# Chunked attention and two MLPs on one core: B and C loaded without their zeros, and the early work in a new order

## The chip, the core and the metric

The kernel runs on one core of one Trainium2 chip. Its time is the device time of one execution in microseconds (us). The core has TensorE (PE, and PEld for its weight loads), VectorE (DVE), ScalarE (ACT), GpSimd (POOL) and SyncE (SP). Most transfers between memory and the core are issued by SP, two early ones by ACT; each engine works through its own list in order.

## What is computed

Four sequences of 768 positions with 8 heads go through a decaying attention in chunks (reference, with chunks of 32), and its output through two MLPs.

```python
cum = np.cumsum(log_a_chunk, axis=-1)
L = np.exp(cum[:, :, :, None] - cum[:, :, None, :]) * causal
M = np.einsum('bhin,bhjn->bhij', Cc, Bc) * L
y[:, :, sl] = einsum(M, xc) + einsum(Cc, state) * exp(cum)[..., None]
state = exp(sum(la)) * state + sum over j of (Bc xc exp(cum_last - cum_j))
# x: (3072, 256) from y
h = x @ moe_w_in;  g = max(h, 0) + log1p(exp(-|h|));  x = g @ moe_w_out      # softplus
h = x @ moe2_w_in; g = where(h >= 1, h, where(h <= -1, 0, (h + 1)**2 / 4));  out = g @ moe2_w_out
```

## The kernel before

**Attention.** A unit u is one chunk of 128 positions of one sequence, all heads; chunk c holds the four units 4c to 4c + 3, and there are 6 chunks. For a pair of units `load_bc` brings one tile `bc` [128, 768]: 256 columns of B, then 512 columns in which C stands beside zeros. A row is one (head, n) of the 16 state entries, even rows belong to one of two heads that share a row group (e = 0), odd rows to the other (e = 1). The zeros make one matrix product in `scores_of` (L1155) give the products of both heads apart: a row adds to its own head's half and nothing to the other's. There are three buffers `bc`, taken in turn, and twelve loads of 384 KB, each by one DMA of 128 rows.

In chunk 0 the decay L of a unit is made by two matmuls (`spread`, L1115, L1116) and an exponential on ACT (`decay`, L1125); DVE multiplies it into the scores (`weigh`, L1179); POOL makes the inputs of the state (`sources`, L1131); PE then forms the unit's output and state (`out`, L1236, L1257); ACT and DVE split the output into a high and a low part (`evac`, L1289, and `ready`, L1297). In the later chunks the decay comes from a scan on DVE (L1123) over rows that were stored and loaded back (`rows`, L1093: 64 partitions per DMA, 256 KB), four units go together, and the running state is scaled by `dec`, a small table that ACT stores to memory (`store_runs`, L1072) and loads back spread over partitions (`dec`, L1100) for the second chunk.

**Weights.** They come as raw 64-bit numbers in pieces of 512 KB (`load_w`, L780), named (m, kind, j): MLP m, kind i or o (`w_in`, `w_out`), j from 0 to 7. Below i0 is (0, i, 0), o1 is (0, o, 1). The pieces are turned into float32 by `w0` (scale of the upper word, L792 to L796), `w1` (the three low bits and more, L804 on ACT), `w2` (L816 joins them on DVE), `w3` (sign, L828; not for i0, i1, o0, o1, whose `w0` is a Prelu on ACT that keeps the sign), then split into a high part (`w_hi`, L733 on ACT or L735 on DVE) and a low part (`split_w`, L966). If `w1` is on DVE, it is a shift of w0's result (L810), and `w2` is another form (L821).

**MLP.** Step s of MLP 0 takes 128 columns of the hidden layer for a whole chunk, or 256 for half a chunk in the first four steps: `up` (L1327 to L1329, three products), the gate `g` on ACT (L1422, before it once a table load, L1421), and `down` (L1451 in the first eight steps, L1463 later, where g is split too). The Prelu of i0, i1, o0, o1 must come before the table load.

**What sets the order.** `program()` lists all jobs with engine, cost in ns, due time, needs and buffers; `Jobs.order` is a list scheduler that puts them in one order, and every engine gets its part of it. Numbers steer it: costs, `RUSH` (ns by which a job is made more or less urgent), `LOW_DVE` (pieces whose `w1` is on DVE), `RUNS` (what the second half of `runs`, DVE's input to the `dec` table, waits for). Where the list leaves PE a gap in the first 26 us, filling matmuls of zeros are put in (L1494 ten at the start, L1545 later); they count as busy time.

A DMA's completion semaphore is one of eight that are used in turn, over both issuing queues: an issue waits until the transfer eight issues back has landed.

Of the kernel before, what the change touches and what calls it, by code (L numbers as in the profile page):

```python
# [14 lines left out]
NB, H, S, D, N = 4, 8, 768, 32, 16  # L15
Q = 128
HALF = 64
NC = S // Q
NU = NC * NB
# [4 lines left out]
PE, ACT, DVE, POOL, SP = "PE", "ACT", "DVE", "POOL", "SP"  # L24
# [3 lines left out]
class Jobs:  # L28
# [12 lines left out]
    def add(self, name, engine, cost=None, due=None, needs=(), takes=(), gives=(), size=0):  # L41
        assert name not in self.jobs, name
        options = engine if isinstance(engine, dict) else {engine: cost}
        takes = [t if isinstance(t, tuple) else (t,) for t in takes]
        self.jobs[name] = (options, due, [n for n in needs if n is not None], takes, list(gives), size)
# [198 lines left out]
def program():  # L244

    jobs = Jobs()
    add = jobs.add
# [36 lines left out]
    for u in range(NU):  # L284
        c, b = divmod(u, NB)
        if u % 2 == 0:
            add(("load_bc", u // 2), SP, 400, takes=["bc"], size=393e3)
        add(("load", u), SP, 400, takes=["u"], size=262e3)
        if c == 0:
            for hg in range(2):  # L290
# [252 lines left out]
}  # L543
TOGETHER = (1, 2, 3, 4, 5)
BT = 4
RUNS = [('ready', 1)]
WEIGH_POOL = []
PRELU = (2, 2)
LOW_ACT = 1
LOW_DVE = set()  # L550
PRE_FROM = 3
BIAS = {DVE: 400, POOL: 500}
PATIENCE = 0
# [21 lines left out]
N_G = 3  # L575
BEHIND = 500.0
RUSH = {
    ("cd", 7): -1000, ("decay", 5): -16000, ("load_w", 1, "i", 2): -16000, ("w1", 0, "o", 1): 16000, ("weigh", 2, 0): -16000,
}
WARM = 10  # L580
LULL = 5
# [6 lines left out]
def tile_kernel(ctx: ExitStack, tc: tile.TileContext, a0, al, bc, ub, w_in, w_out, w2_in, w2_out, out):  # L588
# [7 lines left out]
    nc = tc.nc  # L596
# [146 lines left out]
    def mine(*name):  # L743

        if name[0] in DTYPES:
            if name not in made:
                tag, i = got[name][0]
                made[name] = new(f"{tag}{i}", DTYPES[name[0]], tag)
            return [made[name]]
        return [buf(*b) for b in got[name]]  # L750
# [323 lines left out]
    @job  # L1074
    def load_bc(engine, v):

        nc.sync.dma_start(mine("load_bc", v)[0], bc[v])

    @job
    def load(engine, u):  # L1080
# [64 lines left out]
    def cb_t(u, hg):  # L1145
        bank = buf(*got["scores", last_of(u) // 2][u % 2 * 2 + hg])
        return bank[:, 256:512] if u // NB in TOGETHER and u % NB > 1 else bank
# [7 lines left out]

    def scores_of(v):

        t = mine("load_bc", v)[0]
        for p in range(2):
            for q in range(4):  # L1160
                r = slice(32 * q, 32 * q + 32)
                if 2 * v >= NB:
                    for s in range(2):
                        o = slice(HALF * s, HALF * s + HALF)
                        nc.tensor.matmul(
                            cb_t(2 * v + q // 2, q % 2)[o, p * 128:(p + 1) * 128], t[r, p * 128 + s * HALF:][:, :HALF],
                            t[r, 256 + p * 256 + s * 128:][:, :128], start=True, stop=True,
                        )
                    continue
                nc.tensor.matmul(  # L1170
                    cb_t(2 * v + q // 2, q % 2)[:, p * 256:(p + 1) * 256], t[r, p * 128:(p + 1) * 128],
                    t[r, 256 + p * 256:512 + p * 256], start=True, stop=True,
                )

    @job
# [307 lines left out]
    def finish_lo(engine, m, c, e):  # L1483
        nc.vector.tensor_tensor(
            out=xl[c][:, e], in0=mine("down", root[m, c])[e], in1=xh[c][:, e].bitcast(F32), op=ALU.subtract
        )


    with tc.manual_schedule():
        nc.scalar.preload_act_table_set("natural_log_exp_and_others")  # L1490

        nc.vector.memset(idle, 0.0)
        for i in range(WARM):
            nc.tensor.matmul(  # L1494
                buf("h", i % 2).rearrange("p (a b) -> p a b", a=4), idle, idle.unsqueeze(1).to_broadcast([128, 4, 128]),
                start=True, stop=True,
            )
# [31 lines left out]
        for r in (slice(0, HALF), slice(HALF, Q)):  # L1529
            nc.scalar.copy(eye3[r], one[r, r].unsqueeze(1).to_broadcast([HALF, H, HALF]))  # L1530
        nc.vector.tensor_reduce(
            out=of_one, in_=one.rearrange("p (k e n) -> p e k n", e=2, n=N), axis=mybir.AxisListType.XY, op=ALU.add
        )
        last = 0.0
        for name, engine, slots in order:
            got[name] = slots
# [62 lines left out]
```

## Time and profile before

| | |
|---|---|
| median of 3 runs | 555.11 us (554.71 to 556.46) |
| the profiled execution | 555.7 us, of which the span of its instructions 553.9 us |
| busy, share of the span | PE 99%, PEld 80%, DVE 79%, ACT 71%, POOL 7% |
| granted clock of TensorE | 0.999 of full speed |
| `bc` loads | 12 of 384 KB |
| DMA over the span | 116 GB/s |

Times below are us from the start of the span. An instruction's length overlaps that of the next one on its engine somewhat, so a sequence is measured from start to start. "[0.89 <-ACT gh L1422]" behind a row says that the engine stood idle for 0.89 us before it, and what released it. A busy PE may be filling matmuls.

### The profile page before, as it was taken

To read this page: it belongs to the slowest core of one execution; us is meant where nothing else is said; L and a number is where in the kernel's file an instruction comes from. 1 tells how busy PE (TensorE), PEld (TensorE's weight loads), DVE (VectorE), ACT (ScalarE), POOL (GpSimd) and SP (SyncE) were. 2 spreads that over 40 slices of the span, in tenths; PEclk is the share of its full clock that TensorE was granted. 3 is DMA by queue.
4 is the path that set the end of the run, shared out by engine and by line. 5 is a ranking of instruction groups with operands and counts; after the bars stand their busy time and mean duration, and the time that the engine had idled before them with its cause. 6 is when DMAs were issued, how large, how long until landed. Compare 5 with 4: busy or idle time off the path is not lost.

```text
span 553.9 us, 10465 instructions
## 1 busy us (share of the span) xinstructions
PE 547.3 (99%) x4001; PEld 442.8 (80%) x4001; DVE 437.5 (79%) x817; ACT 391.1 (71%) x719; POOL 38.8 (7%) x44
## 2 busy tenths in 40 slices
PE   9999999999999999999999999999999999999997
PEld 4777878888888888888888888888888888888885
DVE  7889899798856899876687898989886665876663
ACT  7969655636456667665666989786988875988783
POOL 4023110000000100001300000021310000000000
PEclk9999999999999999999999999999999999999999
DMA  7996458567232500376337324514100001100002
GB/s 271 392 238 198 130 179 235 165 213 219 90 133 76 181 1 1 113 253 227 111 116 233 108 77 145 179 38 149 44 1 0 2 0 38 39 0 1 1 1 76
DMA packets 34679, 64.73 MB, mean 117 GB/s; under 512 B 3684, under 2 KB 8164, under 8 KB 34628
## 3 DMA queue, kind: packets, MB, share of 16 engines
q1 hardware_dynamic: 34276, 63.65, 35.8%
q8 instruction: 31, 0.51, 0.4%
q10 hardware_dynamic: 352, 0.41, 0.3%
q14 instruction: 20, 0.16, 0.1%
HBM read 47.61 MB, written 16.43 MB: 116 GB/s over the span
## 4 chain that ended last, share of the span: by engine, by line
PE 93%; DMA 2%; DVE 2%; ACT 1%; SPq 1%; issue 1%; DVEq 0%; ACTq 0%
PE acc L1463 45%; PE h L1334 5%; PE h L1335 5%; PE h L1336 5%; PE z L1334 4%; PE z L1335 4%; PE z L1336 4%; PE h L1327 4%; PE h L1329 4%; PE h L1328 4%; PE acc L1451 3%; PE y L1236 1%; DMA st<-in_w_in_dram 1%; PE y L1268 1%; DMA u<-in_ub_dram 1%; PE z L1329 1%
## 5 line engine op out<-in xcount | busy, mean ns | idle before, releaser
L1437 DVE TENSOR_TENSOR gl<-g,gh 128x512 fp32r<-128x512 f32 x182 | 127.5, 705 | 55.0 <-PE acc L1463 31.1
L1463 PE MATMUL acc<-gh,woh 128*128 128x512 f32 x368 | 144.3, 392 | 0.0
L1463 PE MATMUL acc<-gh,wol 128*128 128x512 f32 x368 | 143.3, 389 | 0.0
L733 ACT CAST gh<-g 128x512 fp32r<-128x512 f32 x171 | 106.2, 621 | 26.4 <-PE acc L1463 14.2
L1463 PE MATMUL acc<-gl,woh 128*128 128x512 f32 x368 | 113.5, 389 | 0.0
L1463 PEld LDWEIGHTS acc<-gh,woh 128*128 128x128 f32 x368 | 69.1, 188 | 15.3 <-issue 0.7
L1463 PEld LDWEIGHTS acc<-gl,woh 128*128 128x128 f32 x368 | 69.1, 188 | 14.4
L1463 PEld LDWEIGHTS acc<-gh,wol 128*128 128x128 f32 x368 | 69.1, 188 | 14.1
L1422 ACT ACTIVATE g<-h 128x512 f32<-128x512 f32 x61 | 36.5, 598 | 52.5 <-PE h L1329 36.6
L1414 ACT ACTIVATE t<-t 128x512 f32<-128x512 f32 x96 | 60.9, 634 | 1.9
L1327 PE MATMUL h<-xh,wih 128*128 128x512 f32 (+1 forms) x114 | 45.8, 402 | 0.0
L1328 PE MATMUL h<-xh,wil 128*128 128x512 f32 (+1 forms) x114 | 42.8, 376 | 0.0
L1329 PE MATMUL h<-xl,wih 128*128 128x512 f32 (+1 forms) x114 | 42.8, 376 | 0.0
L1123 DVE TENSOR_TENSOR_SCAN ld<-ld,eye_t 128x512 f32<-128x512 f32 x20 | 26.5, 1364 | 2.2 <-DMA ld<-clip_z 2.2
L1407 ACT ACTIVATE t<-h 128x512 f32<-128x512 f32 x37 | 22.1, 598 | 7.5 <-PE h L1336 6.5
L1426 DVE TENSOR_TENSOR g<-h,t 128x512 f32<-128x512 f32 x37 | 25.3, 685 | 1.1 <-ACT t L1414 0.3
L1407 ACT ACTIVATE t<-z 128x512 f32<-128x512 f32 x35 | 21.0, 599 | 7.1 <-DVE g L1426 3.9
L1327 PEld LDWEIGHTS h<-xh,wih 128*128 128x128 f32 x114 | 21.5, 188 | 5.3 <-issue 1.1
L1426 DVE TENSOR_TENSOR g<-z,t 128x512 f32<-128x512 f32 x35 | 24.0, 686 | 1.5 <-ACT t L1414 0.5
L1328 PEld LDWEIGHTS h<-xh,wil 128*128 128x128 f32 x114 | 21.4, 188 | 4.6 <-issue 0.7
L1329 PEld LDWEIGHTS h<-xl,wih 128*128 128x128 f32 x114 | 21.4, 188 | 4.1
L1422 ACT ACTIVATE g<-z 128x512 f32<-128x512 f32 x19 | 11.4, 598 | 17.0 <-PE z L1336 8.5
(326 smaller groups left out, 1011.5 us busy)
## 6 DMA issues: line engine op xcount, KB each, us to landing
st<-in_w_in_dram SPq DMA_DIRECT2D x15, 512.0 KB, 5.2
st<-in_w_out_dram SPq DMA_DIRECT2D x15, 512.0 KB, 6.3
u<-in_ub_dram SPq DMA_DIRECT2D x24, 256.0 KB, 6.6
ld<-clip_z SPq DMA_DIRECT2D x20, 256.0 KB, 6.2
bc<-in_bc_dram SPq DMA_DIRECT2D x12, 384.0 KB, 5.7
pre_i<-st_plain SPq DMA_DIRECT2D x15, 256.0 KB, 2.0
pre_s<-st_plain SPq DMA_DIRECT2D x14, 192.0 KB, 5.9
pre_o<-st_plain SPq DMA_DIRECT2D x10, 256.0 KB, 2.5
```

The lines of the kernel that those rows point to most:

```text
L733: nc.scalar.copy(out, in_)
L1327: nc.tensor.matmul(o, wh, xh[c][:, k, t0:t0 + n], start=(k == 0), stop=False)
L1328: nc.tensor.matmul(o, wl, xh[c][:, k, t0:t0 + n], start=False, stop=False)
L1329: nc.tensor.matmul(o, wh, xl[c][:, k, t0:t0 + n], start=False, stop=(k == 1))
L1334: nc.tensor.matmul(bank, wh, bh, start=start, stop=False, skip_group_check=True)
L1335: nc.tensor.matmul(bank, wl, bh, start=False, stop=False, skip_group_check=True)
L1336: nc.tensor.matmul(bank, wh, bl, start=False, stop=True, skip_group_check=True)
L1414: nc.scalar.activation(out=t, in_=t, func=AF.Square, scale=0.5 / SAT, bias=0.5)
L1422: nc.scalar.activation(out=g, in_=ph, func=AF.Softplus)
L1426: nc.vector.tensor_tensor(out=g, in0=ph, in1=t, op=ALU.max)
L1437: engines[engine].tensor_tensor(out=mine("g_lo", s)[0], in0=mine("g", s)[0], in1=mine("g_hi", s)[0].bitcast(F32), op=ALU.subtract)
L1463: nc.tensor.matmul(acc_t(s, e), w, g[:, j * n:(j + 1) * n], start=(begins(e, j) and g is gh and i == 0), stop=(fc + j == NFC - 1 and g is ...
```

## The change

The array of B and C is built without zeros: for each pair of units there are two blocks of 64 rows, C then B for the rows with e = 0, B then C for those with e = 1. `load_bc` is two DMAs of 64 rows x 512 columns (128 KB each), the first into the even rows, columns 0 to 511, the second into the odd rows, columns 256 to 767. So B stands in the middle third of the tile, C of the one head in the first and of the other in the last third. `clear` zeroes the outer thirds of all rows of each of the three buffers once, ahead of its first load: buffer 0 on DVE behind the first instruction, buffer 1 on DVE behind the set-up work, buffer 2 on POOL. The moving operand of the scores takes the outer thirds (0:3:2). The scheduler's numbers are new: cost and size of `load_bc`, `RUNS`, `LOW_DVE`, `RUSH`.

```diff
-            add(("load_bc", u // 2), SP, 400, takes=["bc"], size=393e3)
+            add(("load_bc", u // 2), SP, 800, takes=["bc"], size=262e3)
...
-RUNS = [('ready', 1)]
+RUNS = [('ready', 0)]
...
-LOW_DVE = set()
+LOW_DVE = {(0, 'i', 1), (0, 'i', 5), (0, 'i', 6), (0, 'o', 1), (0, 'o', 3)}
...
-    ("cd", 7): -1000, ("decay", 5): -16000, ("load_w", 1, "i", 2): -16000, ("w1", 0, "o", 1): 16000, ("weigh", 2, 0): -16000,
+    ("decay", 5): -16000, ("load_w", 1, "i", 2): -16000, ("up", 4): 16000, ("w1", 0, "i", 7): -2000, ("w_hi", 0, "i", 2): -8000,
...
     def load_bc(engine, v):
 
-        nc.sync.dma_start(mine("load_bc", v)[0], bc[v])
+        t = mine("load_bc", v)[0].rearrange("(r e) f -> e r f", e=2)
+        for e in range(2):
+            nc.sync.dma_start(t[e][:, 256 * e:256 * e + 512], bc[v, e])
...
-        t = mine("load_bc", v)[0]
+        t = mine("load_bc", v)[0].rearrange("r (k f) -> r k f", k=3)
...
-                    cb_t(2 * v + q // 2, q % 2)[:, p * 256:(p + 1) * 256], t[r, p * 128:(p + 1) * 128],
-                    t[r, 256 + p * 256:512 + p * 256], start=True, stop=True,
+                    cb_t(2 * v + q // 2, q % 2)[:, p * 256:(p + 1) * 256], t[r, 1, p * 128:(p + 1) * 128],
+                    t[r, 0:3:2, p * 128:(p + 1) * 128], start=True, stop=True,
...
+    def clear(engine, i):
+        engine.memset(buf("bc", i).rearrange("r (k f) -> r k f", k=3)[:, 0:3:2], 0.0)
...
         nc.vector.memset(idle, 0.0)
+        clear(nc.vector, 0)
...
+        clear(nc.vector, 1)
+        clear(nc.gpsimd, 2)
         last = 0.0
```

On ACT, between the last output copy of unit 1 and the first gate, before (st1_137 holds o0, st2_138 i1, st3_139 o1; L794 is `w0`, L804 `w1`):

```order
L794 ACTIVATE w32_383<-st1_137 128x512
L804 ACTIVATE t_387<-st1_137,low_bias_73 128x512
L794 ACTIVATE w32_327<-st2_138 128x512
L804 ACTIVATE t_406<-st3_139,low_bias_73 128x512
L794 ACTIVATE w32_383<-st3_139 128x512
L804 ACTIVATE g_412<-st2_138,low_bias_73 128x512
L1421 ACT_TABLE_LOAD
L1422 ACTIVATE gh_415<-h1_210 128x512
```

and now:

```order
L794 ACTIVATE w32_390<-st1_137 128x512
L794 ACTIVATE w32_334<-st2_138 128x512
L804 ACTIVATE t_411<-st1_137,low_bias_73 128x512
L794 ACTIVATE w32_390<-st3_139 128x512
L1423 ACT_TABLE_LOAD
L1424 ACTIVATE gh_416<-h1_212 128x512
```

Two `w1`, those of i1 and o1, are no longer there; `w0` of i1 stands ahead of `w1` of o0.

On DVE, in the same stretch, before (L1179 `weigh` of units 2 and 3, L816 `w2`):

```order
L1179 TENSOR_TENSOR ld3_121<-acc1_270,ld3_121 128x512
L1179 TENSOR_TENSOR ld3_121<-h0_208,ld3_121 128x512
L816 SCALAR_TENSOR_TENSOR w32_383<-w32_383,t_387 128x512
L1179 TENSOR_TENSOR ld2_120<-acc2_285,ld2_120 128x512
L1179 TENSOR_TENSOR ld2_120<-acc0_268,ld2_120 128x512
L816 SCALAR_TENSOR_TENSOR w32_327<-w32_327,g_412 128x512
L816 SCALAR_TENSOR_TENSOR w32_383<-w32_383,t_406 128x512
L735 CAST wih1_75<-w32_327 128x512
L792 TENSOR_SCALAR w32_457<-raw_262 128x512
L966 TENSOR_TENSOR wil1_83<-w32_327,wih1_75 128x512
```

and now, one row earlier on (L1181 is `weigh`, L1299 `ready`, L810 the shift of `w1`):

```order
L1299 TENSOR_TENSOR xl0_368<-y1_269,xh0_367 128x2x128
L1181 TENSOR_TENSOR ld2_120<-acc2_291,ld2_120 128x512
L1181 TENSOR_TENSOR ld3_121<-acc1_273,ld3_121 128x512
L1181 TENSOR_TENSOR ld2_120<-acc0_271,ld2_120 128x512
L1181 TENSOR_TENSOR ld3_121<-h0_210,ld3_121 128x512
L810 TENSOR_SCALAR w32_334<-w32_334 128x512
L816 SCALAR_TENSOR_TENSOR w32_390<-w32_390,t_411 128x512
L821 SCALAR_TENSOR_TENSOR w32_334<-st2_138,w32_334 128x512
L810 TENSOR_SCALAR w32_390<-w32_390 128x512
```

The four `weigh` stand together, unit 2 and 3 in turn, and the joins and the two new shifts behind them.

On ACT, around the store and the load of the `dec` table for the second chunk, before (gh is a gate, wih and woh high parts of weights):

```order
L1072 DMA clip_p_200<-more0_148 8x8x64
L733 CAST woh0_90<-w32_383 128x512
L1422 ACTIVATE gh_551<-h0_208 128x512
L804 ACTIVATE t_561<-st1_137,low_bias_73 128x512
L804 ACTIVATE t_564<-st2_138,low_bias_73 128x512
L796 ACTIVATE w32_573<-st2_138 128x512
L1100 DMA dec0_134<-clip_p_200 128x1x512
L1422 ACTIVATE gh_580<-h1_210 128x512
L804 ACTIVATE t_583<-st3_139,low_bias_73 128x512
L796 ACTIVATE w32_586<-st3_139 128x512
```

and now:

```order
L1072 DMA clip_p_200<-more0_148 8x8x64
L796 ACTIVATE w32_492<-st1_137 128x512
L733 CAST wih3_77<-w32_472 128x512
L1424 ACTIVATE gh_567<-h1_212 128x512
L1102 DMA dec0_134<-clip_p_200 128x1x512
L804 ACTIVATE t_577<-st2_138,low_bias_73 128x512
L733 CAST woh0_90<-w32_390 128x512
L1424 ACTIVATE gh_584<-h0_210 128x512
L733 CAST woh1_91<-w32_390 128x512
L733 CAST woh2_92<-w32_492 128x512
```

The store has kept its place; the load stands two rows earlier among other work, ahead of `w1` of i4 (t_577; before t_564) and of the high parts of o0 to o3, and behind one gate more (567 is that of the fifth step, which is 580 in the list before and stands behind the load there).

On PE the fills between the first step and the outputs of units 2 and 3 go from 7 to 1, the first `down` has three steps of `up` behind it where it had two, and from then on each `up` stands one `down` earlier than before, up to the step at which the ninth and tenth `up` stood together; behind some 450 of 3,100 rows the lists agree again. On SP, the loads of rows for the second chunk (L1093) now stand ahead of the load of o4. On POOL the four low parts of o0 to o3 follow each other, and one product of MLP 0 more comes behind them.

## Rows read from the trace of the kernel before

**Rows 1.** Busy time in stretches: us from the start, length, busy time (instructions) per engine, clock, DMA share, GB/s.

```profile
5.00:10.00 5.00, 5.00 (x32) 2.41 (x30) 4.06 (x9) 3.76 (x9) 1.16 (x4) 1.00 0.88 299
...
15.00:20.00 5.00, 4.69 (x67) 2.70 (x65) 3.57 (x7) 4.22 (x7) 0.00 (x0) 1.00 1.05 394
...
30.00:35.00 5.00, 5.00 (x23) 4.11 (x22) 3.19 (x7) 3.03 (x6) 0.00 (x0) 1.00 0.92 198
...
60.00:80.00 20.00, 19.52 (x383) 15.89 (x374) 18.64 (x38) 11.26 (x22) 3.46 (x2) 1.00 0.74 213
```

**Rows 2.** PE in order of time: start, length, engine, line, operation, count, [idle before <- releaser].

```profile
15.59 1.69 PE L1545 MATMUL y<-idle 128*128 128x512 bf16 x7
...
18.44 1.25 PE L1545 MATMUL acc<-idle 128*128 128x512 bf16 x5
20.58 1.99 PE L1451 MATMUL acc<-gh,w 128*128 128x256 f32 x8 [0.89 <-ACT gh L1422]
...
42.83 0.39 PE L1328 MATMUL h<-xh,wil 128*128 128x512 f32 x1
...
77.33 0.80 PE L1236 MATMUL y<-ld,u 64*32 64x64 f32 x60 [0.48 <-DVE ld L1179]
```

**Rows 3.** ACT in order of time, up to the first gate.

```profile
10.15 0.77 ACT L804 ACTIVATE t<-st,low_bias 128x512 uint32<-128x512 uint32 x1
...
16.59 0.77 ACT L804 ACTIVATE t<-st,low_bias 128x512 uint32<-128x512 uint32 x1 [0.71 <-DMA st<-in_w_out_dram]
17.26 0.68 ACT L794 ACTIVATE w<-st 128x512 f32<-128x512 f32 x1
17.85 0.77 ACT L804 ACTIVATE g<-st,low_bias 128x512 uint32<-128x512 uint32 x1
18.64 1.28 ACT L1421 ACT_TABLE_LOAD   x1
19.93 0.60 ACT L1422 ACTIVATE gh<-h 128x512 f32<-128x512 f32 x1
```

**Rows 4.** SP, the queue that issues the loads, in order of time.

```profile
1.61 0.41 SPq L1077 DMA_DIRECT2D bc<-in_bc_dram  x1
...
3.48 0.43 SPq L780 DMA_DIRECT2D st<-in_w_in_dram  x1
...
15.23 0.38 SPq L780 DMA_DIRECT2D st<-in_w_in_dram  x1
```

**Rows 5.** DVE in order of time, 1 to 21 us.

```profile
1.52 0.79 DVE L1511 CAST eye<-ld 128x128 bf16<-128x128 f32 x1 [0.52 <-POOL ld L1501]
...
3.58 0.23 DVE L997 TENSOR_SCALAR first<-first 128x128 f32<-128x128 f32 x1 [0.49 <-DMA first<-in_a_dram]
...
14.15 0.68 DVE L1179 TENSOR_TENSOR ld<-acc,ld 128x512 f32<-128x512 f32 x1
...
15.95 1.28 DVE L1179 TENSOR_TENSOR ld<-acc,ld 128x512 f32<-128x512 f32 x2
...
20.20 0.42 DVE L792 TENSOR_SCALAR w<-raw 128x512 f32<-128x512 f32 x1
```

**Rows 6.** ACT and DVE around the decay load of the second chunk.

```profile
L1100 ACTq EVENT_SEMAPHORE  x1: 3145/3145/3145, 29.2 to 29.2; - x1
...
33.10 0.60 ACT L1422 ACTIVATE gh<-h 128x512 f32<-128x512 f32 x1 [1.97 <-issue]
...
34.92 0.69 DVE L816 SCALAR_TENSOR_TENSOR w<-w,t 128x512 uint32<-128x512 uint32 x1 [1.80 <-ACT w L796]
35.53 2.30 DVE L1123 TENSOR_TENSOR_SCAN ld<-ld,eye_t 128x512 f32<-128x512 f32 x1
...
38.34 2.33 DVE L1123 TENSOR_TENSOR_SCAN ld<-ld,eye_t 128x512 f32<-128x512 f32 x2
```

**Rows 7.** POOL in order of time: a clearing write, and a product beside DVE.

```profile
1.71 0.52 POOL L1510 MEMSET dec<- 48x512 f32 x1
...
35.47 1.28 POOL L966 TENSOR_TENSOR wol<-w,woh 128x512 fp32r<-128x512 f32 x1 [6.00 <-ACT woh L733]
```

More of the change, by code (lines that the diff above doesn't have):

```diff
@@ L1165, in scores_of @@
                         nc.tensor.matmul(
-                            cb_t(2 * v + q // 2, q % 2)[o, p * 128:(p + 1) * 128], t[r, p * 128 + s * HALF:][:, :HALF],
-                            t[r, 256 + p * 256 + s * 128:][:, :128], start=True, stop=True,
+                            cb_t(2 * v + q // 2, q % 2)[o, p * 128:(p + 1) * 128], t[r, 1, p * 128 + s * HALF:][:, :HALF],
+                            t[r, 0:3:2, p * 128 + s * HALF:][:, :, :HALF], start=True, stop=True,
                         )
@@ L1570 @@
     by_g = lambda v: v.reshape(NB // 2, 2, 2, 2, 2, NC, Q, N).transpose(5, 0, 1, 2, 4, 7, 3, 6)
-    cz = np.zeros((NC, NB // 2, 2, 2, 2, N, 2, 2, Q), x.dtype)
-    for e in range(2):
-        cz[:, :, :, :, e, :, :, e] = by_g(C.reshape(NB, H, NC, Q, N))[:, :, :, :, e]
-    late = cz[1:].reshape(NC - 1, NB // 2, 2, 2, 2, N, 2, 2, 2, HALF)
-    cz[1:] = late.transpose(0, 1, 2, 3, 4, 5, 6, 8, 7, 9).reshape(cz[1:].shape)
-    bc = np.ascontiguousarray(np.concatenate(
-        [by_g(B.reshape(NB, H, NC, Q, N)).reshape(NU // 2, 128, 256), cz.reshape(NU // 2, 128, 512)], axis=2
+    bg, cg = (by_g(v.reshape(NB, H, NC, Q, N)).reshape(NU // 2, 4, 2, N, 256).transpose(2, 0, 1, 3, 4).reshape(2, NU // 2, 4 * N, 256) for v in (B, C))
+    bc = np.ascontiguousarray(np.stack(
+        [np.concatenate([cg[0], bg[0]], axis=2), np.concatenate([bg[1], cg[1]], axis=2)], axis=1
     ))
```

## Prediction

> **What bounds the kernel now.** I read the busy times by stretch first, then PE in order of time, then the engines that PE waits for. The stretches show PE full to the end of nearly every one of them; between 60 and 80 us it lacks 0.48 us, and that is one wait, at 77.33 [rows 1, 2]. So behind the start-up PE walks through a fixed list of products, which the change does not shorten, and the end moves by what PE's list is moved. The busy time of the first 20 us deceives: in PE's own order the rows at 15.59 and 18.44 are twelve filling products on zeros, and behind them PE stands idle for another 0.89 us before the first `down` at 20.58, released by the first gate on ACT [rows 2]. What the change can win is therefore the time by which that first `down` comes earlier; what it can lose is a wait further on, if the engines that feed PE don't come earlier too.
>
> On ACT the gate at 19.93 is the end of a chain without a gap: ACT waits 0.71 us until the second piece of w_out, o1, has landed at 16.59, then come `w1` (0.67 from start to start), `w0` (0.59), one more `w1` (0.79) and the table load (1.29) [rows 3]. On DVE, beside it, the last `weigh` of units 2 and 3 ends at 17.23 [rows 5], and the outputs that need it end where the second row of fills begins, at 18.44 [rows 2], 1.2 us later.
>
> **The loads.** A `bc` load shrinks from 393 KB to 262 KB. From 15 to 20 us the transfers run at 394 GB/s [rows 1], so 131 KB are 0.33 us; two such loads stand ahead of o1, and it lands 0.66 us earlier, at 15.9. The price is twelve more issues on SP of 0.41 us [rows 4]. Only two come ahead of o1, and at the first, i0's own issue goes from 3.48 to 3.9. That piece was issued 6.67 us before ACT could use it (3.48 to 10.15) [rows 3, 4]: most of this is queueing behind other transfers, which covers the 0.41. At 299 GB/s [rows 1] its queue is 0.44 us shorter, but ACT itself is free only some 0.2 us before 10.15, and that much I count at most. Ends for the whole term: 0.9 us (both loads at 299 GB/s) and below nothing (the first rival). I take 0.66, since o1 is moved in the stretch of 394.
>
> The Trainium skill ("SBUF — State Buffer", section "Summary: rules for kernel authors") speaks against this edit: it says to use all 128 partitions in "one DMA, not several". Its section "Door 1: The DMA port swizzle" makes the rate hang on the ports that the partitions reach, and every second row of 128 would still reach all of them. The first rule is the rival of half rate below; by the second, the term stays as it is.
>
> **The clears.** No row shows a DVE clear of 128x512. The nearest are a one-input operation of that size, 0.42 us, of which the next starts 0.33 later (20.20) [rows 5], and POOL's clear of 48x512, 0.52 [rows 7]: 0.3 to 0.6 each. The first falls into the 0.52 us in which DVE waits for POOL, the second into the 0.49 us in which it waits for the first transfer [rows 5]; POOL's stands in a wait of several us. If they fit, they cost nothing; at 0.6, and with POOL's beside DVE's sums, some 0.3 us reach the chain to the `weigh` of units 2 and 3. I take 0.1. The first load now waits for the first clear: behind it on SP stand the loads of a, units 0 and 1 and i0. It was issued at 1.61 [rows 4], about when the clear ends: nothing, or 0.1 us in the queue's cover.
>
> **The first gate.** On ACT the two `w1` leave the chain: o1 at 15.9, `w0` 0.59, table 1.29, and 0.65 from gate to PE (19.93 to 20.58): 18.4 [rows 2, 3]. On DVE the join between the `weigh` goes behind them: four in a row from 14.15 at 0.60 each (the two at 15.95 take 1.28) end at 16.55 instead of 17.23 [rows 5]. The outputs can start when the first unit's are done and end at 17.2; the five fills that stay, 1.25 us [rows 2], end at 18.45. With 0.1 for the clears the first `down` starts at 18.6: a lead of 2.0 us. It can hardly be more than 2.2, since both chains arrive together.
>
> **Does the lead last?** DVE gets five shifts at 0.33 (1.7 us) for five `w1` on ACT, and by the lists up to the second chunk's first `ready` also one split and one join more (0.6 each, as 34.92 to 35.53 [rows 6]) and three casts of 0.34 fewer: +1.9 us, with 2.0 less to do it in. It had idle time enough until 35 us (3.19 busy of 5.00 from 30 to 35 [rows 1]), none after. So the question is where it idles now, and that is the `dec` load on ACT. Before, ACT's queue waited there 3.15 us from 29.2, until the store landed at 32.35; the next gate ran at 33.10, and DVE stood still for 1.80 us until 34.92 [rows 6]. Now the load stands two rows earlier while ACT is 2 us ahead, so the wait grows; behind it are `w1` of i4, four casts and the gates, and DVE's whole list waits for that `w1`. The store's landing hangs on what was issued before it. At the latest it is 32.4, as before; at the earliest 30.7, since five `bc` loads ahead of it save 655 KB, 1.66 us at 394 GB/s. The row loads, which run in the stretch of 198 GB/s [rows 1], come forward and take part of it back: I take 31.5.
>
> From there: 0.75 to ACT's next instruction (32.35 to 33.10), `w1` 0.67 and 0.05, join 0.61, scan 1.2, `w3` 0.6, two scans 2.33, three small products 0.6 (0.2 each, as the 128x128 at 3.58), split and way to PE 0.7: 7.5 us, so the low part of i4 is there at 39.0 [rows 3, 5, 6]. The first scan took 2.30 instead of 1.2 when a product of POOL began at 35.47, just ahead of it [rows 6, 7]; the cast that frees POOL's product stands right behind `w1` again, so this happens again more likely than not: 40.1. PE wants that part at 42.83 before, 22.25 us behind the first `down`; now one `down` fewer stands between (1.99 at most) [rows 2], so at 18.6 + 20.3 = 38.9. Late by 0.1 or 1.2; I take 0.5, since at 31.5 the landing is a middle and an early store absorbs the collision. Further on DVE has no slack for more, but the same half microsecond covers it. Ends of this term: 0 (store at 30.7, no collision: 38.2) and 3.2 (32.4 and two collisions: 42.1).
>
> The Trainium skill ("DMA: Bandwidth & Descriptors", section "Queues, rings and completion order") has each engine take turns between SP's and ACT's rows packet by packet, so ACT's small store should not queue behind SP's megabytes. The 3.15 us wait says otherwise here; by the rule there would be no late term, and the time would be that of the full lead.
>
> The later `bc` loads are smaller in stretches where PE waits 0.48 us in all [rows 2]: nothing to win beyond that, and PE's lead moves that wait along. The scores read their zeros at another place, with as many columns: nothing.
>
> **Sum.** 2.0 − 0.5 = 1.5 us off the profiled execution's 555.7 (its span 553.9 and 1.8 around it): 554.2. That execution lies 0.6 above the median of the runs, 555.11, so 553.6. This is 0.27%, under the 0.3% or so (1.7 us) that a measurement of this kernel can tell from no change.
>
> **Rivals.**
> Full lead: the store lands early, or nothing collides, and PE never waits: 2.0 us, 553.1. For it: DVE's idle time before 35 us. Against: ACT's 3.15 us at the store.
> Half rate: 64 rows per DMA run at the 198 GB/s of the row loads, which also have 64 rows [rows 1]. Then 262 KB take 1.32 us instead of 393 KB in 1.0, o1 lands 0.65 later, at 17.25, and the `down` starts at 17.25 + 0.59 + 1.29 + 0.65 = 19.8: lead 0.8, no late term, 554.3. Against: these rows lie over all partitions, the row loads over one half.
> Slower: the wait at the `dec` load takes over. One mechanism: store lands, ACT's `w1`, DVE's list, low part of i4. The lead is gone when that part comes 2.0 after 38.9, so with one collision at a store of 32.3, with two at 31.2. At 33.0 with two it comes at 42.7, 3.8 late: 1.8 slower, 556.9. For it: the row loads now all stand ahead. Against: 655 KB fewer.
> The change doesn't do what it says: the clears push the early chain so far (over 1 us) that the gate's earlier release is of no use: 555.0.
>
> **Chances.** Forecast 0.34, full lead 0.32, half rate 0.14, slower 0.13, no effect 0.07. Faster by over 0.3% is under 553.4: nearly all of the full lead (0.30) and the upper part of the forecast (0.10), 0.40. Slower by over 0.3%, above 556.8: half of the slower case, 0.07. The rest, 0.53. The range reaches from 552.8 (lead 2.2 and a run that favours it) to 556.0, into the slower case; the forecast's own is 553.3 to 554.2.
>
> **What would show it.** Right: the first `down` at 18.4 to 18.9, o1's `w0` behind a wait that ends near 15.9; ACT's queue at the `dec` load for 3 to 4 us until 31 to 32; a PE wait of about half a microsecond before the low part of i4 near 39, and PE in step from there. Wrong: `bc` halves that take as long as the whole did; a wait of PE over 1.5 us between 35 and 60; a later chain of waits that starts at a scan or a `weigh`.

## The result, and the profile after

The kernel after takes 562.88 us in the median (561.85 to 565.1), the kernel before 555.11 beside it: a ratio of 1.0139, 95% interval 1.0109 to 1.0169, so 7.8 us slower. The profiled execution is at the median: 562.88 us, span 561.2, 7.2 more than the span before (561.16 against 553.93 unrounded); TensorE's mean granted clock is 0.994 of full speed (0.999 before).

The stretches of the kernel after, with the columns of [rows 1]:

```profile
15.00:20.00 5.00, 4.89 (x68) 3.42 (x66) 4.62 (x10) 4.95 (x10) 0.00 (x0) 1.00 1.00 368
...
30.00:35.00 5.00, 5.00 (x21) 3.74 (x20) 1.39 (x3) 1.15 (x2) 0.00 (x0) 1.00 1.01 243
35.00:40.00 5.00, 4.02 (x12) 1.80 (x10) 5.00 (x4) 2.96 (x7) 4.80 (x3) 1.00 0.38 115
40.00:45.00 5.00, 0.73 (x2) 0.42 (x3) 5.00 (x7) 3.46 (x7) 2.44 (x2) 0.83 0.86 274
45.00:50.00 5.00, 5.00 (x10) 2.91 (x10) 5.00 (x13) 3.91 (x7) 0.00 (x0) 0.50 0.41 143
```

Two things stand out. From 39 to 45 us PE has hardly anything to do, while DVE is full; before that, from 30 to 35 us, DVE and ACT were nearly idle. And from 45 to 50 us PE is busy at a granted clock of 0.50. PE in order of time, to be held against [rows 2]:

```profile
18.28 1.99 PE L1453 MATMUL acc<-gh,w 128*128 128x256 f32 x8
...
37.16 1.88 PE L1453 MATMUL acc<-gh,w 128*128 128x512 f32 x4
41.01 0.50 PE L1329 MATMUL h<-xh,wih 128*128 128x512 f32 x1 [1.98 <-ACT gh L1424]
44.77 0.79 PE L1330 MATMUL h<-xh,wil 128*128 128x512 f32 x1 [3.25 <-DVE wil L966]
...
47.06 3.38 PE L1453 MATMUL acc<-gh,w 128*128 128x512 f32 x4
```

The first `down` comes 2.3 us earlier than before. Then the ninth step waits 1.98 us for a gate and 3.25 us for the low part of i4, and the next `down` lasts 3.38 us where the one before took 1.88. What PE waited for, on ACT, DVE, POOL and SP:

```profile
15.61 0.71 ACT L794 ACTIVATE w<-st 128x512 f32<-128x512 f32 x1
...
28.42 0.60 ACT L1424 ACTIVATE gh<-h 128x512 f32<-128x512 f32 x1
32.72 0.69 ACTq L1102 DMA_DIRECT2D dec<-clip_p  x1
33.85 0.76 ACT L804 ACTIVATE t<-st,low_bias 128x512 uint32<-128x512 uint32 x1 [4.83 <-DMA clip_p<-more]
...
39.20 0.62 ACT L733 CAST wih<-w 128x512 fp32r<-128x512 f32 x1 [2.04 <-DVE w L828]
...
40.39 0.57 ACT L1424 ACTIVATE gh<-h 128x512 f32<-128x512 f32 x1
```
```profile
34.64 0.69 DVE L816 SCALAR_TENSOR_TENSOR w<-w,t 128x512 uint32<-128x512 uint32 x1 [3.30 <-ACT t L804]
35.25 2.31 DVE L1125 TENSOR_TENSOR_SCAN ld<-ld,eye_t 128x512 f32<-128x512 f32 x1
37.48 1.69 DVE L828 SCALAR_TENSOR_TENSOR w<-st,w 128x512 uint32<-128x512 uint32 x1
39.09 4.43 DVE L1125 TENSOR_TENSOR_SCAN ld<-ld,eye_t 128x512 f32<-128x512 f32 x2
43.45 0.66 DVE L1133 TENSOR_TENSOR bt<-u,ld 128x128 f32<-128x128 f32 x3
44.03 0.68 DVE L966 TENSOR_TENSOR wil<-w,wih 128x512 fp32r<-128x512 f32 x1
```
```profile
35.20 7.25 POOL L966 TENSOR_TENSOR wol<-w,woh 128x512 fp32r<-128x512 f32 x4 [21.37 <-ACT woh L733]
```
```profile
1.61 1.16 SPq L1079 DMA_DIRECT2D bc<-in_bc_dram  x2
...
4.38 0.43 SPq L780 DMA_DIRECT2D st<-in_w_in_dram  x1
...
32.69 5.20 SPq L1072 DMA_DIRECT2D clip_p<-more  x4
37.99 0.40 SPq L780 DMA_DIRECT2D st<-in_w_in_dram  x1
```

ACT computes nothing for 4.83 us: up to 32.65 it stands at the `dec` load, until the store of the run table has landed, and 1.2 us go from there to the start of `w1`. `w1` of i4 is behind the load, and so is all of DVE's list. The casts of o0 to o3 stand behind it too, so POOL gets its four products at once and runs them from 35.20 to 42.45, beside everything that DVE now has to do. The gate that PE waits for (40.39) hangs on the same list: it stands on ACT behind the cast at 39.20, which waits for DVE's `w3` at 37.48. The load of i5 is issued at 37.99; in the trace of before it was 35.18. At the other end o1's `w0` runs at 15.61, straight behind `w1` of o0 and not behind a wait for o1, and i0 is issued at 4.38 against 3.48 [rows 4].

### The profile page after: what moved, and what is told of

Its sections match the earlier page's. It is cut to its first block, busy times and chain, and to the rows that moved or that the text cites. A ratio compares the mean times of both kernels' runs of the same rounds, so it can differ in the third digit from the quotient of the medians.

```text
span 561.2 us, 10477 instructions
## 1 busy us (share of the span) xinstructions
PE 549.7 (98%) x3995; PEld 443.2 (79%) x3995; DVE 440.6 (79%) x820; ACT 390.4 (70%) x718; POOL 39.6 (7%) x45
## 3 DMA queue, kind: packets, MB, share of 16 engines
HBM read 46.04 MB, written 16.43 MB: 111 GB/s over the span
## 4 chain that ended last, share of the span: by engine, by line
PE 89%; DMA 4%; ACT 2%; issue 2%; DVE 2%; SPq 0%; ACTq 0%; DVEq 0%
PE acc L1465 44%; PE h L1336 5%; PE h L1338 5%; PE h L1337 5%; PE z L1336 4%; PE z L1338 4%; PE z L1337 4%; PE h L1329 4%; PE h L1330 4%; PE h L1331 4%; DMA st<-in_w_in_dram 2%; DMA clip_p<-more 1%; PE y L1238 1%; PE y L1270 1%; PE z L1330 1%
## 5 line engine op out<-in xcount | busy, mean ns | idle before, releaser
L1331 PE MATMUL h<-xl,wih 128*128 128x512 f32 (+1 forms) x114 | 43.3, 380 | 0.0
L1125 DVE TENSOR_TENSOR_SCAN ld<-ld,eye_t 128x512 f32<-128x512 f32 x20 | 28.8, 1476 | 2.9 <-DMA ld<-clip_z 2.9
```

Source lines behind the costliest of these rows:

```text
L1331: nc.tensor.matmul(o, wh, xl[c][:, k, t0:t0 + n], start=False, stop=(k == 1))
```

## Experiments

Medians; the ratio is to the kernel before on the same chip, with its 95% interval. "Whole" loads are those of before.

| kernel | loads | order | us | ratio |
|---|---|---|---|---|
| loads_alone | split | before | 557.97 | 1.0054 (1.0037 to 1.0072) |
| split_full | split, with zeros | before | 557.91 | 1.0041 (1.0022 to 1.0059) |
| one_load | one DMA, no zeros | before | 554.83 | 0.9992 (0.9978 to 1.0005) |
| order_alone | whole | new | 561.87 | 1.0123 (1.0108 to 1.0139) |
| order_both | whole | new, both moves | 555.18 | 0.9998 (0.9982 to 1.0013) |
| dec_late | split | new, `dec` moved | 559.15 | 1.0069 (1.0053 to 1.0084) |
| lows_late | split | new, low parts moved | 561.21 | 1.0105 (1.009 to 1.012) |
| both_late | split | new, both moves | 557.11 | 1.0046 (1.0025 to 1.0066) |
| fills | split | new, fills at 39 us | 561.29 | 1.0115 (1.01 to 1.013) |

**The two halves apart.** loads_alone is the kernel after with the old numbers of the scheduler (`RUNS`, `LOW_DVE`, `RUSH`, cost and size of `load_bc`), order_alone the kernel before with the new ones.

> The kernel after with the scheduler's numbers of the kernel before: B and C in halves without zeros, buffers cleared once, all lists in the order of before. Theory (the new order does the harm, the loads and clears none): o1 lands 0.5 to 1 us earlier than 16.59, but the two w1 still stand on ACT behind it, so the first down comes at 19.6 to 20.3 instead of 20.58; no wait of PE over 1 us behind 30 us, clock at 0.99 or more of full speed throughout; 554 to 555.5 us. Rival (the half loads run at half their rate or the clears hold up the early chain, and this starts the late wait): the first down at 20.6 or later, or a wait of PE over 2 us between 35 and 50 us, and 557 us or more.

> The kernel before (B and C with zeros, one load of 128 rows, no clears) with the new scheduler's numbers, so the lists stand as in the kernel after. Theory (the order does the harm): o1 lands near 16.3 to 16.6 instead of 15.6, the first down stands at 18.9 to 19.6; ACT waits at the dec load from about 29.5 to the landing of the store, 32.3 to 33.2, POOL then makes its four products at a stretch beside DVE's scans, PE waits 4.5 to 6 us between 37 and 46 and its clock falls to half for some microseconds behind that; 562 to 565 us. Rival (the new order is good and the half loads spoil it): PE waits under 2 us in that stretch and the time is 553.5 to 556.

The order alone costs 6.6 us and shows the same picture as the kernel after; PE in order_alone:

```profile
19.12 1.99 PE L1451 MATMUL acc<-gh,w 128*128 128x256 f32 x8 [0.80 <-ACT gh L1422]
...
41.51 0.49 PE L1327 MATMUL h<-xh,wih 128*128 128x512 f32 x1 [1.93 <-ACT gh L1422]
45.27 0.79 PE L1328 MATMUL h<-xh,wil 128*128 128x512 f32 x1 [3.27 <-DVE wil L966]
```

But my theory held the loads to be harmless, and they alone cost 2.7 us (557.97 against 555.25 beside it), by neither of the ways in the rival: the first `down` came early, at 19.41. SP, ACT and PE in loads_alone:

```profile
37.53 0.40 SPq L780 DMA_DIRECT2D st<-in_w_in_dram  x1
```
```profile
41.45 0.77 ACT L804 ACTIVATE t<-st,low_bias 128x512 uint32<-128x512 uint32 x1 [4.05 <-DMA st<-in_w_in_dram]
```
```profile
44.65 1.99 PE L1453 MATMUL acc<-gh,w 128*128 128x512 f32 x4 [1.66 <-ACT gh L1424]
```

i5 is issued 2.4 us later than before, ACT waits 4.05 us for it, and the gate behind it holds PE. The lists tell why: each load of B and C now takes two of the eight completion semaphores, and so i5's issue waits for the semaphore that the `dec` load holds, where it waited for that of the small store before. The trace bears this out: the last update of that semaphore comes at 37.45, and the wait ends at 37.50. (The profile puts the wait down to a low part on DVE that ends at 37.45 too, but by the lists the issue doesn't wait for that one.) Both kernels have the same products on PE in the same order, so they can be held against each other product by product: loads_alone is 1.2 us ahead up to this gate, 0.7 behind from it on, and 1.9 behind at 57 us, by further waits for low parts.

**The second issue, or the fewer bytes?** split_full loads all 768 columns in two halves of the rows; one_load brings 512 columns by one DMA, with C not beside zeros (the scores read other data). In the array of before the 16 rows of a head stand together and not in turn with those of the other, so the even rows of split_full are not one head's; the sums over the rows are the same.

```diff
-            nc.sync.dma_start(t[e][:, 256 * e:256 * e + 512], bc[v, e])
+            nc.sync.dma_start(t[e], rows[e])                                # split_full
+        nc.sync.dma_start(mine("load_bc", v)[0][:, 0:512], bc[v].rearrange("e r f -> (e r) f"))   # one_load
```

> The kernel before, in its own order, with each load of B and C as two DMAs, of the even and the odd rows, with all 768 columns and the zeros: as many bytes as before, no clears, twelve issues more. Theory (the second issue is the price of the new loads: SP feeds the queue later in the first 5 us, and the eight semaphores come round earlier): no byte is saved, so o1 lands at 16.8 to 18 us, the first down stands at 20.8 to 22, the load of i5 is issued at 37 or later instead of 35.2; 557.5 to 560 us. Rival (the issues are covered, and the clears or the fewer bytes do what was measured of the loads alone): 554.5 to 556 us.

> The kernel with the loads and clears alone (order of before), but each load of B and C as one DMA of 128 rows x 512 columns, so C isn't put beside zeros: what the scores read is other data, the sizes of all operations stay. Theory (it is the second issue that costs): o1 lands 0.5 to 1 us earlier than 16.59, i5 is issued near 35, PE waits under 0.7 us behind 25 us; 553.8 to 555 us. Rival (the clears, or that the zeros are not loaded, cost time in themselves): 556.5 to 558.5 as with two DMAs.

With as many bytes as before and no clears, split_full costs what loads_alone does, in the same place (SP, ACT, PE):

```profile
38.37 0.40 SPq L780 DMA_DIRECT2D st<-in_w_in_dram  x1
```
```profile
42.38 0.76 ACT L804 ACTIVATE t<-st,low_bias 128x512 uint32<-128x512 uint32 x1 [3.97 <-DMA st<-in_w_in_dram]
```
```profile
46.25 1.98 PE L1454 MATMUL acc<-gh,w 128*128 128x512 f32 x4 [2.27 <-ACT gh L1425]
```

Product by product, split_full is 0.2 us ahead of the kernel before up to this gate and 2.3 behind from it on; there too the semaphore of the `dec` load is updated last at 38.30, just ahead of i5's issue. one_load issues i5 at 32.41, and PE waits nowhere behind the first `down`; it has the clears and is not slower. So the second issue is the price, not the clears, and not that the halves run slowly: from 15 to 20 us split_full moves 397 GB/s, against 394 before [rows 1]. That one_load is 0.3 us faster is within what can be told from nothing.

**The two hold-ups of the order.** dec_late and lows_late undo one each, both_late both, order_both both with whole loads.

```diff
+    behind(("dec", 1), ("w_hi", 0, "o", 3))                      # the load, on ACT behind the casts of o0 to o3
+    for j, other in enumerate([("ready", 5), ("ready", 7), ("weigh", 11, 1), ("g_lo", 17)]):
+        behind(("split_w", 0, "o", j), other, DVE)               # low parts of o0 to o3 from POOL to DVE, 60 to 80 us
```

> The kernel after, with the load of the dec table for chunk 1 moved on ACT behind the four casts of o0 to o3; nothing else changes place. Theory (ACT's queue at the dec load starts the wait of PE): w1 of i4 runs at 29.5 to 31.5 instead of 33.85, DVE's join 0.8 us behind it, the first scan when the rows have landed (31.5 to 32.5); POOL's four products still run beside the scans, so the low part of i4 is there at 40.5 to 42 instead of 44.7 and PE waits 1.5 to 3 us in place of 5.2. If the clock then still falls to half, 558 to 560 us; if it doesn't, 555.5 to 557.5. Rival A (POOL's products alone hold DVE up, the start doesn't matter, since DVE waits for its rows anyway): the low part of i4 stays at 43.5 or later, 561.5 to 563. Rival B (the late store, not its place in ACT's list, decides through another path, such as SP's lists behind its own stores): the same 561.5 to 563, with the wait now before another tile.

> The kernel after, with the low parts of o0 to o3 taken from POOL and made on DVE between 60 and 80 us, where they are not yet needed; the dec load stays where it is. Theory (of the 10 us from DVE's join at 34.64 to the low part of i4 at 44.7, some 4 are the products of POOL that run beside DVE): the scans take 1.2 us each instead of 2.2 and the sign step 0.7 instead of 1.7, the low part of i4 is there at 40.3 to 41, PE waits 1.2 to 2 us instead of 5.2; if the clock still falls to half, 558 to 559.5 us; if it doesn't, 555.5 to 557. Rival (the scans are slow for another reason, such as rows that land late): scans of 2 us and more stay with an idle POOL beside them, and the time is 562 to 564.

dec_late took 559.15 us, as expected with a clock that falls (0.91 in the mean from 35 to 55 us). `w1` of i4 runs when its piece has landed, but POOL's products still lie beside the scans (ACT, DVE, PE):

```profile
30.97 0.78 ACT L804 ACTIVATE t<-st,low_bias 128x512 uint32<-128x512 uint32 x1 [1.97 <-DMA st<-in_w_in_dram]
```
```profile
36.31 4.46 DVE L1125 TENSOR_TENSOR_SCAN ld<-ld,eye_t 128x512 f32<-128x512 f32 x2
```
```profile
42.01 0.51 PE L1330 MATMUL h<-xh,wil 128*128 128x512 f32 x1 [2.95 <-DVE wil L966]
```

In lows_late the same scans, without POOL, take half:

```profile
36.07 0.69 DVE L816 SCALAR_TENSOR_TENSOR w<-w,t 128x512 uint32<-128x512 uint32 x1 [4.16 <-ACT t L804]
36.68 1.22 DVE L1125 TENSOR_TENSOR_SCAN ld<-ld,eye_t 128x512 f32<-128x512 f32 x1
37.81 0.67 DVE L828 SCALAR_TENSOR_TENSOR w<-st,w 128x512 uint32<-128x512 uint32 x1
38.39 2.33 DVE L1125 TENSOR_TENSOR_SCAN ld<-ld,eye_t 128x512 f32<-128x512 f32 x2
...
41.23 0.69 DVE L966 TENSOR_TENSOR wil<-w,wih 128x512 fp32r<-128x512 f32 x1
```

From the join to the low part of i4 it is 5.2 us there (36.07 to 41.23) and 9.4 in the kernel after (34.64 to 44.03): POOL's four products cost DVE 4.2 us. The mechanism came out, the time didn't: the clock stayed up, for which I had expected 555.5 to 557 us, and the median is 561.21. The profiled execution, the fastest of four at 559.81, shows a part of the gap: the store landed 1.4 us later (the `dec` load is issued at 34.15 against 32.72), and PE waits 0.91, 1.14, 0.68 and 0.91 us between 36 and 51.

> The kernel after with both moves: the dec load behind the casts of o0 to o3 on ACT, and their low parts on DVE between 60 and 80 us. Theory (late start plus collision make up the whole wait before the low part of i4): w1 of i4 at 31.0, the join at 31.9, the first scan at 32.9 when its rows have landed, scans of 1.2 us, the low part of i4 at 38.3 to 38.9, about when PE wants it, so PE waits under 0.5 us there and the clock stays; behind it PE still waits 1 to 2 us for the low parts of i5 or i6, since i5's load is issued at 35 behind the four stores of run tables; 554.5 to 557 us. Rival (there is a third hold-up behind the two, of the same size): PE waits over 2 us before the low part of i4 or more than 3 us up to 60 us, 558 or more.

> The loads of the kernel before (whole, with zeros, one DMA) in the new order, with both moves: the dec load on ACT behind the casts of o0 to o3, their low parts on DVE between 60 and 80 us. Theory (the order's harm of 6.7 us is the two things moved, and the rest of the 2.0 us by which the kernel with both moves and the split loads is slower than before belongs to the split): the first down at 18.9 to 19.8, no wait of PE over 1 us behind it, clock at 0.998 or more; 554.3 to 556 us. Rival (the new order costs 1.5 to 2 us more elsewhere, by the five shifts that it adds to DVE): 556.5 to 558 us, with waits of PE for DVE between 40 and 60 us or near 80.

Of the 7.8 us both moves together win 5.8 with split loads (557.11, at the edge of what was expected), and with whole loads all of the order's 6.6: order_both is equal to before. Its low part of i4 is made at 36.95, and PE's longest wait behind the first `down` is 0.8. So the order's harm is these two things, and the 2.0 us that both_late still loses belong to the split loads. Where they go is open: in the two profiles both_late is behind order_both by 2.0 us at the first `down` already (20.11 against 18.12, o1 having landed late), and the table of first gates below shows no such loss in the mean.

**The clock.** fills puts 24 products of zeros on PE ahead of the ninth step's `up`.

> The kernel after with 24 more filling products of zeros on PE (0.21 us each by the rows of the fills, 5.1 us) ahead of the up of the ninth step, where PE stands idle for 5.2 us in two pieces; nothing else is changed. Theory (the fall of the clock to half from 43.4 to 50.2 us follows from PE's idle stretch, and costs half of the 5.3 us that PE works in it): the granted clock stays at 1.00 from 39 to 52 us, the low part of i4 comes at 44.7 as before, and 2.5 to 3 us are won: 559.7 to 560.6 us. Rival A (the clock falls for another reason): it still falls, 562 to 564. Rival B (the fills push the real products back as far as the clock gives): no change within 0.7 us of 562.9.

The stretch from 35 to 55 us, first in the kernel after, then in fills:

```profile
35.00:55.00 20.00, 14.75 (x39) 8.34 (x38) 19.16 (x28) 13.43 (x25) 7.25 (x4) 0.83 0.56 185
```
```profile
35.00:55.00 20.00, 18.82 (x69) 10.33 (x68) 18.60 (x28) 14.49 (x25) 7.34 (x4) 1.00 0.66 188
```

The clock stays at its upper level (2.4 GHz) and 1.6 us are won, less than the 2.5 expected. The profiles show why. In this execution the store landed 1.7 us later (the `dec` load is issued at 34.41), so the product that uses the low part of i4 ran at 46.56, 1.8 us later than in the kernel after; at 49.77 fills is 0.75 us ahead. So the clock gave back 2.5 us, and the later store took 1.8 of them; of the executions that weren't profiled no row tells this.

**Attempts at a faster version.** loads_stores is loads_alone with the four stores of run tables for later chunks on SP behind the loads of i5, o5 and i6; act_halves is that with the second halves of the first two loads issued by ACT; all_late and order_all are both_late and order_both with those stores moved; order_fill is order_both with two of the low parts at 38 us.

```diff
+    for c in (5, 4, 3, 2):
+        behind(("store_runs", c), ("load_w", 0, "i", 6))
...
-            nc.sync.dma_start(t[e][:, 256 * e:256 * e + 512], bc[v, e])
+            (nc.scalar if v < 2 and e else nc.sync).dma_start(t[e][:, 256 * e:256 * e + 512], bc[v, e])   # act_halves
...
+    for j, other in enumerate([("w2", 0, "o", 4), ("split_w", 0, "o", 0), ("ready", 5), ("ready", 7)]):  # order_fill
```

> The kernel with the loads and clears alone (order of before, 557.97 us), and the four stores of run tables for the later chunks stand on SP behind the loads of i5, o5 and i6. Theory (twelve more issues turn the eight semaphores so that i5's load waits for the landing of the dec load, issued 37.53 instead of 35.18, which costs the lead of 1.2 and 1.6 to 2.8 us more): i5 is issued at 31.3 to 33, ACT's wait of 4.05 us at 41.45 goes, PE waits under 0.7 us up to 60 us, and the lead of 1.2 stays: 553.5 to 554.7 us. Rival (the half loads delay i5 in the queues, whatever its issue): ACT still waits over 2 us for i5, 556.5 to 558.5.

It took 558.07 us (1.0058, 1.0043 to 1.0074). i5 is issued at 33.96 and PE waits nowhere behind 21 us; but the first `down` of the profiled execution came at 20.98, and the clock fell behind that wait (PE, and the stretch from 20 us):

```profile
20.98 2.95 PE L1453 MATMUL acc<-gh,w 128*128 128x256 f32 x8 [1.89 <-ACT gh L1424]
```
```profile
20.00:35.00 15.00, 14.03 (x73) 12.67 (x74) 12.33 (x22) 10.59 (x24) 1.53 (x1) 0.89 0.91 283
```

Product by product it is 2.0 us behind the kernel before at 25 us, by the first gate and the clock, and loses nothing more up to 60 us, where loads_alone lost 3.1 and split_full 2.4. So an early i5 does take that loss away, but the time doesn't show it.

> The loads and clears alone in the order of before, with the four stores of run tables behind i5, o5 and i6 on SP, and the second halves of the first two loads of B and C issued by ACT instead of SP. Theory (the late feeding of the queue in the first 5 us eats what the fewer bytes give): SP issues i0 at 3.5 instead of 4.4, o1 lands at 15.3 to 16.2, the first down stands at 19.3 to 20.2, no wait of PE over 0.7 us follows; 553.8 to 555 us, so not slower than before. Rival (o1's landing scatters by a microsecond or more whatever is issued first): the first down at 20.5 or later, 556.5 to 558.5 us.

> As the last one, and the four stores of run tables for the later chunks stand on SP behind the loads of i5, o5 and i6. Theory (SP's list, held at the stores, is what makes i5 late): i5 is issued at 31.5 to 33.5 instead of 38 and ACT doesn't wait for it; PE's waits from 35 to 60 us come to under 1 us in all; a part of the lead of 2.3 us is left at 60 us, 553.5 to 555.5 us. Rival (DVE, which is full from 35 us on in every run, sets the low parts of i5 and i6, not their loads): PE's waits stay as in the kernel with both moves, and so does the time within 0.7 us.

> Whole loads, the new order and both moves (555.18 us), and the four stores of run tables for the later chunks stand on SP behind the loads of i5, o5 and i6. Theory (what is left of the lead of 2.3 us is lost behind 38 us because i5's load comes late: ACT waits 1.34 us for it and DVE 1.25): i5 is issued near 31 instead of 32.8, those waits go, PE's wait of 0.8 us too, 554 to 554.9 us, so 0.3 to 1 us faster than before. Rival (DVE is full there and takes the time back in any order): within 0.3 us of 555.2. Rival B (the earlier half-megabytes push the landing of the run table's store for chunk 1 back, as in the kernels where this was done with split loads): 555.5 to 557.

> Whole loads, the new order and both moves, but the low parts of o0 and o1 on DVE at 38 us, where DVE stood idle for 1.25 us, and those of o2 and o3 between 60 and 70 us. Theory (DVE's idle time at 38 us is free, and 1.2 us less work between 70 and 80 us takes away PE's wait of 0.4 us near 84): 554.5 to 555.0 us. Rival (DVE's list behind 39 us is pushed back by up to 1.2 us where PE already waits): PE's wait for low parts up to 50 us grows to 1 to 2 us, 555.3 to 556.5.

None beats the kernel before: act_halves took 557.25 (1.0037, 1.0013 to 1.006), all_late 557.78 (1.0049, 1.0035 to 1.0064), order_all 556.54 (1.0027, 1.0015 to 1.004), order_fill 555.32 (1.0003, 0.9991 to 1.0015). In act_halves the first `down` stands at 19.63 as expected, but the store lands later (`dec` load at 33.73) and the gate behind it holds PE for 1.25 us. In all_late and order_all PE waits for DVE near 56 and 78 us (1.3 and 1.2 us together), so there the rival comes nearer, that DVE takes the time back.

**How steady is the first gate?** before_again is the kernel before, profiled once more.

> The kernel before, profiled a second time. Theory (the landing of o1 scatters by some tenths with whole loads, by 2 us with the halves, which reached from 15.4 to 17.5 in eight profiles): o1 at 16.2 to 17.0, the first down at 20.2 to 21.0, the store of the run table for chunk 1 lands at 32 to 33. Rival (it scatters as much with whole loads): o1 before 16.0 or behind 17.2.

It took 555.06 us, with o1 at 15.90, 0.7 earlier than in [rows 3] and outside what I expected of whole loads. ACT's table load, which ends the chain to the first gate, starts at the times below in all profiles but two, whose first loads are issued otherwise (one_load 17.99, act_halves 17.68):

| order | whole loads | split loads |
|---|---|---|
| before | 18.64, 17.94 | 17.47, 18.47, 19.03 |
| new | 15.96, 16.31, 17.18, 17.66 | 16.34, 16.43, 16.81, 16.87, 17.03, 18.17 |

It scatters by up to 1.8 us between kernels whose early lists are alike, and by 0.7 between two executions of the kernel before. The new order brings it 1.5 us forward in the mean (18.3 to 16.8), and the split loads bring nothing that shows in this scatter (16.8 against 16.9).

## Why the prediction was wrong

**The loads, 0.66 us: wrong, though the profile after seemed to bear it out.** o1's `w0` ran at 15.61 there; but that is one draw from the scatter above, and ACT didn't wait for o1. The step that failed is, as far as is known, "this is queueing behind other transfers, which covers the 0.41": i0 is issued 0.90 later and not 0.42, so the queue is fed later and carries less from 3 to 5 us, first before, then after:

```profile
3.00:5.00 2.00, 2.00 (x6) 0.60 (x4) 1.07 (x5) 0.66 (x2) 1.26 (x3) 1.00 0.99 299
```
```profile
3.00:5.00 2.00, 2.00 (x6) 0.59 (x4) 1.08 (x4) 0.66 (x2) 1.79 (x4) 1.00 0.84 214
```

These 0.17 MB are two thirds of the 262 KB that two loads save ahead of o1. The other profiles show the same: 203 to 227 GB/s in the eight in which SP issues all the halves without zeros, 265 and 267 in split_full and act_halves, 288 to 308 in the seven with one DMA for a load. That it is what eats the gain is argued, not shown. The rival of half rate was wrong too: split_full has the halves at full size, and its o1 landed at 16.44 (16.59 and 15.90 before).

**The later loads, "nothing to win": I looked only for a gain.** Their twelve issues also turn the semaphores, and i5's load is issued 2.4 to 3.2 us later (loads_alone, split_full). In the kernel after the last of SP's four stores of run tables waits 3.9 us for the `dec` load in this way, and i5 stands behind it. Alone the split costs 2.7 us (both medians); the prediction named the eight semaphores ahead of it and did not count them.

**The clears, 0.1: right. The first gate, 18.6: met, in part by luck.** one_load bears out the clears; the first `down` came at 18.28, and at 19.12 and 18.12 with whole loads. But 0.66 of the 2.0 us of lead were the loads', and by the table above the gain is the order's, 1.5 in the mean.

**The late term, 0.5 with an upper end of 3.2: the step that decided.** Its mechanism is the one that the prediction described (and gave 0.13 as the slower rival): store lands, ACT, DVE's list, low part of i4. Its size was wrong in three places. The store landed at 32.65, where I took 31.5 and allowed 32.4: five smaller loads did not bring it forward at all, and with the same early lists it landed later still in lows_late and fills (`dec` load at 34.15 and 34.41). From the store to `w1` it is 1.2 us (32.65 to 33.85), not 0.75. And I priced one collision with POOL at 1.1 us, from a place where POOL had one product [rows 7], though the list showed four behind each other, all released by the casts that wait behind the same load: they cost 4.2. Together 39.0 + 1.2 + 0.45 + 4.2 = 44.85; the product that uses the low part ran at 44.77. PE's two waits up to there come to 5.2 us.

**The clock: a term that was missing.** [rows 1] shows 1.00 all through, and I took that for given. In the kernel after it falls to 0.50 (the level of 1.2 GHz) in PE's second wait and stays there from 43.3 to 50.1 us, and PE works 5.3 us in it: some 2.6 us lost at half the rate. fills got back 1.6 in the median and 2.5 in its profile.

**The sum** is then −2.3 + 5.2 + 2.6 = 5.5 of the 7.2 us by which the span grew. Measured from start to start the two waits cost 5.7 us and not 5.2: the last product of the `down` at 37.16 starts at 38.44 and the next two at 41.01 and 44.77, where 0.43 and 0.23 lie between such products without a wait. That makes 6.0. Held against the kernel before, PE is 6.3 us behind at 62.75 us, where the lists agree again, and 6.3 at 89 us; the wait of 0.42 us at 83.63 adds nothing, since before had one of 0.48 at 77.33 [rows 2]. Of the rest 0.6 comes between 250 and 410 us, and 0.27 behind the start of PE's last product. For the 0.6, and for the 0.3 that are missing up to 62 us, I have no row. The i5 load is in this sum only so far as it makes the waits above longer.

**The rule on engines that take turns** between SP's and ACT's rows (the Trainium skill, "DMA: Bandwidth & Descriptors", section "Queues, rings and completion order") was rightly not followed: the store was issued at 25.03 and landed 7.6 us later. But the trace doesn't speak against taking turns as such: the packets of ACT's queue moved from 28.9 to 31.3, beside those of SP. Why none moved in the 3.9 us before that, no row shows.

## What to carry to other kernels

A change that issues more transfers is priced by its issues, not by its bytes: each one delays the queue behind it and moves every later issue to another completion semaphore, so look up for each issue near the critical path whose landing it will then wait for. Where an engine waits for a landing, list everything that stands behind the wait on it: what is released together will run together, and products on POOL beside DVE's operations can cost DVE more (4.2 us for four) than if it made them itself (0.6 each). A lead at the start is worth only what the engines behind it can keep up with (order_both has its first `down` 2.5 us earlier than before and the same time), and a single profile of a start that hangs on transfers is one draw out of a microsecond or two.

## What the hardware showed beside that

Every kernel with split loads needs 0.25 us more from the start of PE's last product to the end of its span: 4.7 us in the ten of them, 4.4 in the seven with one DMA for a load. The last transfer of the output has landed 3.6 us behind that product in all of them. But SP waits for the semaphores one after the other, and its wait for this transfer, the last, has become the long one (us in all, times, longest; before, then after):

```profile
SPq L1594 <- DMA out_dram<-dec_plain: 0.3, 1, 0.3
```
```profile
SPq L1598 <- DMA out_dram<-dec_plain: 2.0, 1, 2.0
```

Before, SP waits for this transfer's semaphore at the end. With twelve issues more the transfer holds the semaphore that SP waits for first, and four waits of 0.06 us each stand behind it.

And a wait of PE does not always bring the clock down, nor does its length alone decide: in loads_stores it fell behind a wait of 1.89 us, in split_full it stayed at 1.00 behind one of 2.27, in both_late behind one of 1.60, and in lows_late behind several of 0.7 to 1.1.
